# Layer 2's weight loads on GpSimd's queue, and two engines ordered by the scheduler, beside layer 1 of a three-stage kernel

## The chip, the cores and the metric

The kernel runs on one core of a Trainium2 chip. The core has five engines with an instruction stream of their own each: TensorE (PE in the rows: matmuls; PEld is its weight load), VectorE (DVE), ScalarE (ACT), GpSimd (POOL) and SyncE (SP). Each works through its stream in order. A DMA is put into a queue by an engine (here SyncE or GpSimd) and carried out beside them by the core's DMA engines. The metric is the device time of one execution in microseconds, as the median of three runs; a profile is one further execution.

## The reference

A retention (a linear attention with decay) feeds an expert layer with a gated activation, and that feeds a second expert layer with a rational activation. With the sizes: 4 batches, 8 heads, 768 positions, 64 per head, so 3072 tokens of 512; both layers go from 512 to 2048 and back.

```python
def _attn_ref(q, k, v):
    for t in range(S):
        state = gamma[None, :, None, None] * state + np.einsum('bhd,bhe->bhde', k[:, :, t], v[:, :, t])
        y[:, :, t] = scale * np.einsum('bhd,bhde->bhe', q[:, :, t], state)

def _moe_ref(x, w_in, w_out):            # layer 1
    h = x @ w_in
    g = h * (1.0 / (1.0 + np.exp(-1.702 * h)))
    return g @ w_out

def _moe2_ref(x, w_in, w_out, a, b):     # layer 2
    h = x @ w_in
    h2 = h * h
    P = a[0] + a[1] * h + a[2] * h2 + a[3] * h2 * h
    Q = 1.0 + np.abs(b[0]) * np.abs(h) + np.abs(b[1]) * h2
    return (P / (Q + 1e-06)) @ w_out
```

The inputs are 64-bit floats. The kernel makes a high and a low part of each matrix and adds three products (low times high, high times low, high times high) where the reference has one.

## The kernel before

Layer 1 goes over 6 blocks of 512 tokens, and in a block over 16 chunks f of 128 of the 2048 hidden columns: 96 steps. Step i, written in `step(i)`, does on TensorE first `g1(i+2)`, 12 matmuls into one of two banks hp (L1122), then `g2(i)`, 12 matmuls into four banks o that gather a whole block (L1143 to L1145). So g1 runs two steps ahead. Between them stand ScalarE's z=sigmoid(hp) (L1229), VectorE's z=hp*z (L1230), ScalarE's gh, the high part of z (L1238), and VectorE's gl, the low part (L1239). A bank hp is free again when VectorE's z has read it. After the 16th chunk, `evac` copies the four banks o into two pair tiles `os` (L1153, L1155) and SyncE stores them (L1156); layer 2 reads them back later.

Beside these steps runs other work, hung on the middle or the end of a step:

- Attention units for the chunks of 128 tokens that the later blocks read, 16 of them in steps 16 to 76. `att_unit` does the matmuls pY, pS and pK (L954), ScalarE and VectorE take pY out as xh and xl (L960, L962), VectorE makes the state st and the masked scores sm. What a unit needs is prepared before it: `load_raw` loads rawq, rawk and rawv (L735), `att_turn` scales and transposes q and k on VectorE (L816, L818) and writes them to DRAM as tq and tk (L823), `att_fetch` reads them back as qT and kT (L831). These DMAs, 4 or 2 for each of the seven tiles, are SyncE's. pY takes one of the two hp banks.
- The conversion of layer 2's weights: 32 units of 128 by 1024 words (512 KB), four for each of 8 groups g: u=4g and u+1 from w_in, u+2 and u+3 from w_out. `raw2(u)` loads the two 32-bit words of each number (L629, L631). `word2(u)` makes a 32-bit float of them: ScalarE u<-s (L561, in `w_first`), VectorE u<-u and s<-s (L567, L569), u<-u,s (L572) and u<-s,u (L583). For w_in four sums of quarter blocks follow on VectorE (L682). Each result is split by `split`: ScalarE takes the high part (L619), VectorE the low (L620), and `put` has GpSimd write both to DRAM, where layer 2 fetches them (L655 for w_in, L653 for w_out).

Which step a unit is converted in comes from `conv0`: group g begins at step 18 + 9g, less 0 to 4 for the last groups, and `conv2(g, x)` is called at the end of step i with x = i - conv0[g] from -1 to 9. It loads at x = -1, 0, 3 and 5, and the other pieces are spread over the ten steps.

Three pools set what may overlap. `ws` has 4 slots of 8 KB a partition, tag "s": a raw unit lies in one from its load to its put, the group's sums in one, one w_out result in one, and evac's two os pairs each in one. `ch` has 3, shared by z and the transposed q and k. The hp banks are 2.

The order on an engine is the program's where it is kept, and the scheduler's where not. In steps 14 to 77 TensorE, VectorE, ScalarE and SyncE keep the program's order:

```python
        with tc.manual_schedule(engines={E.PE, E.DVE, E.Activation, E.SP}):
            for i in range(FIRST_STEPS, XS0):   # 14 to 77
                step(i)
        for i in range(XS0, NS):                # 78 to 95
            step(i)
```

GpSimd, which only issues the puts there, is ordered by the scheduler. `behind(dma)` keeps one DMA in the program's order on its queue.

Of the kernel before, what the change touches and what calls it, by code (L numbers as in the profile page):

```python
# [18 lines left out]
P = 128  # L19
# [4 lines left out]
KD = DM // P  # L24
# [447 lines left out]
def tile_kernel(ctx: ExitStack, tc: tile.TileContext, q, k, v, w1i, w1o, w2i, w2o, pa, pb, cst, out):  # L472
    nc = tc.nc
# [47 lines left out]
    def unit(layer, u):  # L521
        return (ORD if layer == 1 else ORD2)[u]

    def stage_tag(u):

        if u < 16:
            at_slot = 31 - u
        elif u < 24:
            at_slot = 47 - u
        elif u < 28:  # L530
            at_slot = 55 - u
        elif u == 30:
            at_slot = 31
        else:
            return None
        return f"w{at_slot}"
# [49 lines left out]
    def w_high(layer, u, whole=True):  # L586
        nm, fc = unit(layer, u)
        if whole and layer == 1 and u in LATER:
            return
        m = STG[u]  # L590
        shape = [P, KD, P] if nm == "i" else [P, DM]
        if nm == "i":
            m = m.rearrange("p (c f) -> p c f", c=KD)
        pair = wp.tile([P, 2, *shape[1:]], F32R, tag=f"w{u}", name=f"w{nm}{layer}_{fc}")
        STG[u] = m
        W[layer, nm, fc] = (pair[:, 0], pair[:, 1])
        high = nc.scalar.copy(out=pair[:, 0], in_=m)
        if not whole:
            tc.keep_in_program_order(high)
# [9 lines left out]
    NG = KF // 2  # L609
# [3 lines left out]
    def behind(dma):  # L613

        tc.keep_in_program_order(dma)
# [6 lines left out]
    def raw2(u):  # L622

        nm, f = unit(2, u)
        src = {"i": w2i, "o": w2o}[nm].bitcast(I32)
        s = ws.tile([P, DM, 2], I32, tag="s", name=f"s2_{u}")
        if nm == "i":
            src = src[:, f * 2 * P : (f + 1) * 2 * P].rearrange("(c p) f -> p c f", p=P)
            behind(nc.sync.dma_start(out=s.rearrange("p (c f) t -> p c (f t)", c=KD), in_=src))  # L629
        else:  # L630
            behind(nc.sync.dma_start(out=s.rearrange("p f t -> p (f t)"), in_=src[f * P : (f + 1) * P, :]))  # L631
        STG[u] = RW[u] = s

    def word2(u):
        w_first(u)
        w_bits(u)
        w_sign(u, False)
# [4 lines left out]
    def parts(key, src, home):  # L642

        n = src.shape[1] // (2 * P)
        t = home.bitcast(F32R).rearrange("p a b -> p (a b)").rearrange("p (x h c) -> p x h c", x=n, h=2)
        split((t[:, :, 0], t[:, :, 1]), src.rearrange("p (x c) -> p x c", c=2 * P))
        OUT2[key] = t

    def put(key):
        t = OUT2.pop(key)  # L650
        g, x = key
        if x == "o":
            nc.gpsimd.dma_start(out=WO[g], in_=t.bitcast(F32))  # L653
        else:
            nc.gpsimd.dma_start(out=WC[g][x].rearrange("x p h k f -> p x (h k f)"), in_=t.rearrange("p x h c -> p x (h c)").bitcast(F32))  # L655

    def whole(f, src, home):
        t = home.bitcast(F32R).rearrange("p a b -> p (a b)").rearrange("p (h c) -> p h c", h=2)
        split((t[:, 0], t[:, 1]), src)
        OUT2[f, "o"] = t  # L660

    def conv2(g, x):

        u = 4 * g
        if x == -1:
            raw2(u)
        elif x == 0:
            raw2(u + 1)
            word2(u)
        elif x == 1:  # L670
            parts((g, 0), STG[u], RW.pop(u))
        elif x == 2:
            put((g, 0))
            word2(u + 1)
        elif x == 3:
            raw2(u + 2)
            a, b = STG.pop(u), STG.pop(u + 1)
            a11, a12, a21, a22 = a[:, : 2 * P], a[:, 2 * P :], b[:, : 2 * P], b[:, 2 * P :]
            t = SUM[g] = ws.tile([P, 4, 2 * P], F32, tag="s", name=f"sum{g}")
            A22S[g] = a22  # L680
            for y, p, q, op in ((0, a21, a22, ALU.add), (1, t[:, 0], a11, ALU.subtract), (2, a11, a21, ALU.subtract), (3, a12, t[:, 1], ALU.subtract)):
                nc.vector.tensor_tensor(out=t[:, y], in0=p, in1=q, op=op)  # L682
            parts((g, 1), t[:, 0:2].rearrange("p x c -> p (x c)"), RW.pop(u + 1))
        elif x == 4:
            put((g, 1))
        elif x == 5:
            raw2(u + 3)
            word2(u + 2)
            t = SUM.pop(g)
            parts((g, 2), t[:, 2:4].rearrange("p x c -> p (x c)"), RW.pop(u + 2))  # L690
            parts((g, 3), A22S.pop(g), t[:, 0:2])
        elif x == 6:
            put((g, 2))
            put((g, 3))
        elif x == 7:
            word2(u + 3)
            e = ws.tile([P, DM, 2], I32, tag="s", name=f"wo{2 * g}s")
            whole(2 * g, STG.pop(u + 2), e)
        elif x == 8:
            put((2 * g, "o"))  # L700
            whole(2 * g + 1, STG.pop(u + 3), RW.pop(u + 3))
        elif x == 9:
            put((2 * g + 1, "o"))
# [409 lines left out]
    def g1(j):  # L1113
        layer, bi, fc, t0, n = steps[j]
        hp = ps_h.tile([P, n], F32, tag="h", name=f"hp{j}")
        wh, wl = W[layer, "i", fc]
        xh, xl = X[layer, bi]
        terms = [(kk, w, x) for kk in range(KD) for w, x in ((wl, xh), (wh, xl), (wh, xh))]
        if j == 0:
            terms.sort(key=lambda t: ((t[2] is xl) + (t[1] is wl or t[2] is xl), t[0]))  # L1120
        for x, (kk, w, t) in enumerate(terms):
            nc.tensor.matmul(hp, w[:, kk, :], t[kk // 2][:, kk % 2, :], start=(x == 0), stop=(x == len(terms) - 1))  # L1122
        HP[j] = hp
# [90 lines left out]
    def load_wo(f):  # L1214
        t = WOT[f] = wp.tile([P, 2, DM], F32R, tag=f"w{14 + f}", name=f"wo{f}t")
        tc.keep_in_program_order(nc.sync.dma_start(out=t.bitcast(F32), in_=WO[f]))
# [7 lines left out]
    def act1_a(j):  # L1224
        n = steps[j][4]
        hp = HP.pop(j)
        z = ch.tile([P, n], F32, tag="z", name=f"z{j}")
        CH[j] = z
        nc.scalar.activation(out=z, in_=hp, func=ACTF.Sigmoid, scale=1.702)  # L1229
        nc.vector.tensor_tensor(out=z, in0=hp, in1=z, op=ALU.mult)  # L1230
# [54 lines left out]
    for u in range(NU):  # L1285
        t = stage_tag(u)
# [9 lines left out]
    E = mybir.EngineType  # L1296
    with tc.manual_schedule(engines={E.SP}):
# [207 lines left out]
        conv0 = [KF + 2 + 9 * g - (0, 0, 0, 0, 1, 2, 3, 4)[g] for g in range(NG)]  # L1505
# [13 lines left out]
        def x_piece(i):  # L1519
            left = 2  # L1520
            while xq and left and (xq[0][0] or i > XS0 + 8):
# [10 lines left out]
                else:  # L1532
                    left -= 1
                    for f in xr[s, kk][n]:
                        if f:
                            f()

        def step(i):
            nonlocal nxt, j
            while nxt < NS and nxt - lead[steps[nxt][0]] <= i:  # L1540
                j = nxt
                nxt += 1
                g1(j)
                act1_a(j)
            if 0 <= i - KF + 2 < WHOLE:
                w_high(1, LATER[i - KF + 2], False)
                w_low(1, LATER[i - KF + 2], False)
            if i == KF:
                tc.keep_in_program_order(nc.scalar.activation(out=ab[:, 6:7], in_=ab[:, 5:6], func=ACTF.Abs))
            late = [f() for f in todo[i][0]]  # L1550
            if j >= FIRST_STEPS + 2 and j in CH:
                act1_b(j)
            for f in late:
                if f:
                    f()
            g2(i)
            layer, bi, fc, t0, n = steps[i]
            if fc == KF - 1 and bi < 5:
                evac(bi)
            late = [f() for f in todo[i][1]]  # L1560

            if i >= XS0:
                x_piece(i)
            if i >= NS - 4:
                load_wo(2 * (i - NS + 4))
                load_wo(2 * (i - NS + 4) + 1)
            if i == XS0 + 4:
                for kk in range(2):
                    t = xp.tile([P, 2, 512], F32, tag=f"xh{kk}_0", name=f"xb{kk}")
                    XB.append(t)  # L1570
                    for c in range(2):
                        nc.sync.dma_start(out=t[:, c], in_=x2[4][2 * c + kk])
            for g in range(NG):
                x = i - conv0[g]
                if x == 9:
                    conv2(g, x)
            for g in range(NG):
                x = i - conv0[g]
                if -1 <= x < 9:
                    conv2(g, x)  # L1580
            for f in late:
                if f:
                    f()

        with tc.manual_schedule(engines={E.PE, E.DVE, E.Activation, E.SP}):
            for i in range(FIRST_STEPS, XS0):
                step(i)
        for i in range(XS0, NS):
            step(i)
# [32 lines left out]
```

## Time and profile before

| what | value |
|---|---|
| median of three runs | 1193.75 us (1192.49 to 1194.94) |
| the profiled execution | 1192.8 us, its span 1191.0 us, mean granted clock 0.971 |
| TensorE busy | 1119.5 us (94% of the span) |
| VectorE busy | 868.8 us (73%) |
| ScalarE busy | 655.2 us (55%) |
| GpSimd busy | 31.1 us (3%) |

The rows that matter stand in the section ahead of the prediction. A row of the stretches gives a window in microseconds from the span's start, its length, and what each engine was busy in it, then the granted TensorE clock as a share of full speed, the share of the DMA engines and GB/s. In the timeline, the figure in brackets is the time in which the engine was idle before the instruction, and what ended it. A wait lists who waited with which tile, for which engine's result or for which DMA, in total, how often, and the longest. Steps 16 to 77 of layer 1 lie between about 140 and 600 us; layer 2 begins past 680 us.

### The profile page before, as it was taken

The numbers are of one execution on the slowest core, as the hardware profiler recorded it, in microseconds if no ns is written. First come the engines' busy times: TensorE is split into PE (matmuls) and PEld (weight loads), VectorE is DVE, ScalarE is ACT, GpSimd is POOL, SyncE is SP. The second block draws the span as 40 slices with busy tenths as digits, with TensorE's granted clock in tenths as the row PEclk, the third lists the DMA queues.
The fourth block names the chain that finished last, engine by engine and source line by source line (L and its number), as shares of the span: only waits on it lengthen the run. The fifth ranks groups of instructions, "written<-read, shape, count | busy, mean of one in ns | idle before, by whom it ended". The sixth has DMA issues, their size and how long they took to land.

```text
span 1191.0 us, 18828 instructions
## 1 busy us (share of the span) xinstructions
PE 1119.5 (94%) x7217; PEld 911.8 (77%) x7217; DVE 868.8 (73%) x1192; ACT 655.2 (55%) x987; POOL 31.1 (3%) x52
## 2 busy tenths in 40 slices
PE   8999999698996879797999999999999999999998
PEld 6688878577775757586888888888888888888887
DVE  6999646375564445455577679999889899789895
ACT  5998322132232322222354569978778786787782
POOL 0000000000000000000000000000000000000000
PEclk9999999889998989899999999999999999999999
DMA  9944557565564554565278798583345561354100
GB/s 238 326 129 115 113 127 164 151 159 153 139 157 133 141 147 120 156 168 160 95 261 297 230 325 286 195 297 153 91 129 153 184 247 46 122 157 122 43 36 36
DMA packets 230394, 193.54 MB, mean 163 GB/s; under 512 B 153888, under 2 KB 178976, under 8 KB 230304
## 3 DMA queue, kind: packets, MB, share of 16 engines
q1 hardware_dynamic: 223904, 169.27, 49.4%
q0 software_dynamic: 6400, 23.07, 5.3%
q8 instruction: 57, 0.93, 0.3%
q14 instruction: 33, 0.27, 0.1%
HBM read 134.48 MB, written 57.67 MB: 161 GB/s over the span
## 4 chain that ended last, share of the span: by engine, by line
PE 66%; SPq 11%; DMA 9%; DVE 5%; issue 3%; ACT 2%; DVEq 0%; ACTq 0%
PE o L256 22%; PE hp L1122 13%; PE a L157 11%; SPq L735 7%; PE c L157 5%; DMA s<-in_moe_w_out_dram 4%; PE o L1143 3%; PE o L1144 3%; PE o L1145 3%; PE b L157 3%; DMA s<-in_moe_w_in_dram 2%; DMA xs<-x 2%; SPq L831 2%; SPq L823 1%; PE pY L954 1%
## 5 line engine op out<-in xcount | busy, mean ns | idle before, releaser
L1122 PE MATMUL hp<-xh,wi 128*128 128x512 f32 x768 | 266.7, 410 | 44.5 <-DVE z L1230 42.8
L1122 PEld LDWEIGHTS hp<-xh,wi 128*128 128x128 f32 x768 | 150.8, 196 | 81.8 <-DVE z L1230 45.9
L1122 PE MATMUL hp<-xl,wi 128*128 128x512 f32 x384 | 154.8, 404 | 0.0
L157 PE MATMUL a<-x,wi 128*128 128x512 f32 x576 | 145.3, 390 | 0.0
L1143 PE MATMUL o<-gh,wo 128*128 128x512 f32 x368 | 144.5, 393 | 0.0
L1144 PE MATMUL o<-gl,wo 128*128 128x512 f32 x368 | 143.6, 390 | 0.0
L1145 PE MATMUL o<-gh,wo 128*128 128x512 f32 x368 | 143.4, 390 | 0.0
L567 DVE TENSOR_SCALAR u<-u 128x512 f32<-128x512 f32 x64 | 27.0, 422 | 139.7 <-ACT u L561 139.7
L561 ACT ACTIVATE u<-s 128x512 f32<-128x512 f32 x64 | 43.1, 675 | 151.7 <-DMA s<-in_moe_w_in_dram 86.7
L157 PEld LDWEIGHTS a<-x,wi 128*128 128x128 f32 x576 | 108.0, 188 | 22.9 <-ACT b L180 0.4
L1238 ACT CAST gh<-z 128x512 fp32r<-128x512 f32 x80 | 49.6, 620 | 99.6 <-DVE z L1230 99.6
L1229 ACT ACTIVATE z<-hp 128x512 f32<-128x512 f32 x80 | 47.6, 595 | 86.3 <-PE hp L1122 80.1
L1230 DVE TENSOR_TENSOR z<-hp,z 128x512 f32<-128x512 f32 x80 | 54.9, 686 | 44.8 <-ACT z L1229 36.7
L1122 PEld LDWEIGHTS hp<-xl,wi 128*128 128x128 f32 x384 | 75.9, 198 | 15.2 <-issue 0.3
L320 DVE SCALAR_TENSOR_TENSOR z<-z,ab,w 128x1024 f32<-128x1024 f32 x48 | 61.6, 1283 | 28.4 <-ACT w L318 28.4
L1143 PEld LDWEIGHTS o<-gh,wo 128*128 128x128 f32 x368 | 69.7, 189 | 15.1 <-DVE wo L605 0.4
L1239 DVE TENSOR_TENSOR gl<-z,gh 128x512 fp32r<-128x512 f32 x80 | 54.7, 684 | 36.1 <-ACT gh L1238 35.0
L1144 PEld LDWEIGHTS o<-gl,wo 128*128 128x128 f32 x368 | 69.4, 189 | 14.6 <-DVE gl L1239 0.2
L1145 PEld LDWEIGHTS o<-gh,wo 128*128 128x128 f32 x368 | 69.2, 188 | 14.5
L157 PE MATMUL c<-x,wi 128*128 128x512 f32 x288 | 73.1, 389 | 0.0
L334 ACT ACTIVATE gh<-h 128x1024 fp32r<-128x1024 f32 x48 | 50.9, 1060 | 34.1 <-PE o L256 33.5
L338 DVE SCALAR_TENSOR_TENSOR gl<-h,gh 128x1024 fp32r<-128x1024 f32 x48 | 58.8, 1224 | 5.4 <-ACT gh L334 5.4
(246 smaller groups left out, 2203.5 us busy)
## 6 DMA issues: line engine op xcount, KB each, us to landing
wi<-wc SPq DMA_DIRECT2D x168, 256.0 KB, 2.9
s<-in_moe_w_in_dram SPq DMA_DIRECT2D x32, 512.0 KB, 5.6
s<-in_moe_w_out_dram SPq DMA_DIRECT2D x32, 512.0 KB, 5.2
x<-xc SPq DMA_DIRECT2D x28, 512.0 KB, 8.5
wc<-s POOLq DMA_DIRECT2D x24, 512.0 KB, 3.9
xc<-xo SPq DMA_DIRECT2D x36, 256.0 KB, 2.7
x<-os SPq DMA_DIRECT2D x20, 256.0 KB, 2.5
xs<-x SPq DMA_DIRECT2D x20, 256.0 KB, 4.3
```

The lines of the kernel that those rows point to most:

```text
L157: nc.tensor.matmul(bank, wt[:, a, k], XT[s, x, k][:, b], start=begin and y == 0, stop=y == 5, skip_group_check=True)
L256: nc.tensor.matmul(ACC[d], a[:, x, r], w[:, b], start=g == 0 and x == 0 and y == 0, stop=g == NG - 1 and x == 1 and y == 2)
L320: dve("q", [("ab", m)], lambda: stt(out=v["z"], in0=v["z"], scalar=ab[:, 6:7], in1=v["w"], op0=ALU.mult, op1=ALU.add))
L334: nc.scalar.activation(out=GT[m][0], in_=h, func=ACTF.Copy, scale=-1.0)
L338: nc.vector.scalar_tensor_tensor(out=gl, in0=h, scalar=-1.0, in1=gh.bitcast(F32), op0=ALU.mult, op1=ALU.subtract)
L735: nc.sync.dma_start(out=t[HALF[n], NP * x : NP * x + NP, :], in_=heads[x])
L1122: nc.tensor.matmul(hp, w[:, kk, :], t[kk // 2][:, kk % 2, :], start=(x == 0), stop=(x == len(terms) - 1))
L1143: nc.tensor.matmul(o, wl[:, r], gh, start=a, stop=False)
L1144: nc.tensor.matmul(o, wh[:, r], gl, start=False, stop=False)
L1145: nc.tensor.matmul(o, wh[:, r], gh, start=False, stop=z)
L1230: nc.vector.tensor_tensor(out=z, in0=hp, in1=z, op=ALU.mult)
L1239: nc.vector.tensor_tensor(out=gl, in0=z, in1=gh.bitcast(F32), op=ALU.subtract)
```

## The change

Three things change, all in steps 14 to 95 of layer 1.

1. `raw2` issues its DMA from GpSimd's queue, no longer from SyncE's. The load calls leave `conv2` and become `conv2_load(g, x)`, called where `conv2` was, at the end of a step.
2. The rest of `conv2` is called by `convert(i - 1)`, right after `g1` and `act1_a` of step i. What was written at the end of step i - 1 is so written early in step i.
3. VectorE and ScalarE leave the list of engines that keep the program's order in steps 14 to 77; the scheduler orders them there. TensorE and SyncE stay in the list.

```diff
@@ raw2
         if nm == "i":
-            behind(nc.sync.dma_start(out=s.rearrange("p (c f) t -> p c (f t)", c=KD), in_=src))
+            behind(nc.gpsimd.dma_start(out=s.rearrange("p (c f) t -> p c (f t)", c=KD), in_=src))
         else:
-            behind(nc.sync.dma_start(out=s.rearrange("p f t -> p (f t)"), in_=src[f * P : (f + 1) * P, :]))
+            behind(nc.gpsimd.dma_start(out=s.rearrange("p f t -> p (f t)"), in_=src[f * P : (f + 1) * P, :]))
@@
+    def conv2_load(g, x):
+        n = {-1: 0, 0: 1, 3: 2, 5: 3}.get(x)
+        if n is not None:
+            raw2(4 * g + n)
+
     def conv2(g, x):
         u = 4 * g
-        if x == -1:
-            raw2(u)
-        elif x == 0:
-            raw2(u + 1)
+        if x == 0:
             word2(u)
...
         elif x == 3:
-            raw2(u + 2)
...
         elif x == 5:
-            raw2(u + 3)
             word2(u + 2)
@@ enter
+        def convert(i):
+            for g in sorted(range(NG), key=lambda g: i - conv0[g] != 9):
+                if 0 <= i - conv0[g] <= 9:
+                    conv2(g, i - conv0[g])
+
         def step(i):
...
                 g1(j)
                 act1_a(j)
+            convert(i - 1)
...
             for g in range(NG):
-                x = i - conv0[g]
-                if x == 9:
-                    conv2(g, x)
-            for g in range(NG):
-                x = i - conv0[g]
-                if -1 <= x < 9:
-                    conv2(g, x)
+                conv2_load(g, i - conv0[g])
...
-        with tc.manual_schedule(engines={E.PE, E.DVE, E.Activation, E.SP}):
+        with tc.manual_schedule(engines={E.PE, E.SP}):
```

TensorE's order is the same in both kernels, and SyncE's is the same without the 32 loads. The number behind z, gh and hp is the step (z35 is that of step 35); u8 and s2_8 are unit 8 of the weights, wc2_0 and wo2 their places in DRAM, sum2 the sums of group 2.

GpSimd in the middle of group 2 (units 8 to 11), before: puts alone.

```order
L653 DMA wo2_137<-wo2s_3270 128x1024
L653 DMA wo3_138<-s2_7_3176 128x1024
L655 DMA wc2_0_111<-s2_8_3308 128x2x512
L655 DMA wc2_1_112<-s2_9_3447 128x2x512
L655 DMA wc2_2_113<-s2_10_3570 128x2x512
L655 DMA wc2_3_114<-sum2_3572 128x512
```

GpSimd at the same place, after:

```order
L653 DMA wo2_137<-wo2s_3286 128x1024
L629 DMA s2_8_3305<-in_moe2_w_in_dram 128x4x256
L629 DMA s2_9_3446<-in_moe2_w_in_dram 128x4x256
L653 DMA wo3_138<-s2_7_3176 128x1024
L655 DMA wc2_0_111<-s2_8_3305 128x2x512
L631 DMA s2_10_3570<-in_moe2_w_out_dram 128x1024
L655 DMA wc2_1_112<-s2_9_3446 128x2x512
L631 DMA s2_11_3758<-in_moe2_w_out_dram 128x1024
L655 DMA wc2_3_114<-sum2_3588 128x512
```

The loads of units 8 to 11 stand among the puts: that of unit 10 behind the put of unit 8, that of unit 11 behind the put of unit 9.

ScalarE from step 36 to 39, before: units 7 and 8 are begun two steps apart.

```order
L1238 CAST gh36_3248<-z36_3245 128x512
L561 ACTIVATE u7_3264<-s2_7_3176 128x512
L619 CAST wo2s_3270<-u6_3178 128x512
L1229 ACTIVATE z37_3286<-hp37_3273 128x512
L1238 CAST gh37_3289<-z37_3286 128x512
L619 CAST s2_7_3176<-u7_3264 128x512
L1229 ACTIVATE z38_3323<-hp38_3310 128x512
L1238 CAST gh38_3342<-z38_3323 128x512
L561 ACTIVATE u8_3449<-s2_8_3308 128x512
L960 CAST xh3_0_3092<-pY_13_3358 128x2x128
L960 CAST xh3_1_3093<-pY_13_3358 128x2x128
L1229 ACTIVATE z39_3478<-hp39_3465 128x512
```

ScalarE from step 34 to 35, after, where these units are now (a line of code has a number one higher from L1230 on in the changed file):

```order
L1230 ACTIVATE z34_3052<-hp34_3039 128x512
L561 ACTIVATE u7_3280<-s2_7_3176 128x512
L1239 CAST gh34_3072<-z34_3052 128x512
L561 ACTIVATE u8_3475<-s2_8_3305 128x512
L619 CAST s2_7_3176<-u7_3280 128x512
L961 CAST xh3_0_3092<-pY_12_3096 128x2x128
L961 CAST xh3_1_3093<-pY_12_3096 128x2x128
L561 ACTIVATE u9_3548<-s2_9_3446 128x512
L619 CAST s2_8_3305<-u8_3475 128x2x256
L1230 ACTIVATE z35_3201<-hp35_3188 128x512
L1239 CAST gh35_3214<-z35_3201 128x512
```

Units 7, 8 and 9 are begun within one step, and unit 9 ahead of z35. The same holds for VectorE, whose work on a unit follows ScalarE's: before, units are spread (u6 in step 34, u7 in 36, u8 in 38, u9 in 40); after, units 7 to 13 stand in steps 34 to 38, units 14 to 21 in 50 to 55, units 22 to 29 in 66 to 71 and units 0 to 6 in 18 to 24, and between these no unit stands.

## Rows read from the trace of the kernel before

**Rows 1.** Four stretches: engines' busy time, PEclk the granted clock, DMA share, GB/s.

```profile
160.00:600.00 440.00, 376.70 (x3294) 309.21 (x3293) 237.75 (x434) 118.30 (x223) 26.51 (x41) 0.92 0.56 147
600.00:690.00 90.00, 89.73 (x396) 73.89 (x395) 63.98 (x108) 44.16 (x76) 4.42 (x8) 1.00 0.77 268
235.00:241.00 6.00, 0.49 (x15) 0.30 (x7) 2.85 (x6) 1.21 (x3) 0.00 (x0) 0.50 0.43 147
241.00:244.00 3.00, 3.00 (x7) 2.42 (x8) 2.93 (x5) 1.62 (x4) 0.00 (x0) 0.50 0.19 44
```

**Rows 2.** Waits of the whole span: total us, times, longest us.

```profile
ACT u L561 <- DMA s<-in_moe_w_in_dram: 86.7, 7, 15.5
...
ACT u L561 <- DMA s<-in_moe_w_out_dram: 62.2, 11, 10.4
...
PE hp L1122 <- DVE z L1230: 42.8, 10, 9.6
...
PE pY L954 <- DVE z L1230: 17.2, 6, 4.1
...
PE pK L954 <- DMA rawv<-in_v_dram: 3.1, 1, 3.1
```

**Rows 3.** ScalarE's timeline: start us, duration us, operation, idle time before and its end.

```profile
237.39 0.66 ACT L561 ACTIVATE u<-s 128x512 f32<-128x512 f32 x1 [14.52 <-DMA s<-in_moe_w_in_dram]
237.95 0.58 ACT L1229 ACTIVATE z<-hp 128x512 f32<-128x512 f32 x1
```

**Rows 4.** SyncE's timeline: issue us, length us of the issues, tile and count.

```profile
216.71 1.78 SPq L823 DMA_DIRECT2D tq<-turnq  x4
...
232.64 1.09 SPq L629 DMA_DIRECT2D s<-in_moe_w_in_dram  x2
```

**Rows 5.** DMA issues of the page: count, KB each, median us to landing.

```profile
s<-in_moe_w_in_dram SPq DMA_DIRECT2D x32, 512.0 KB, 5.6
s<-in_moe_w_out_dram SPq DMA_DIRECT2D x32, 512.0 KB, 5.2
x<-xc SPq DMA_DIRECT2D x28, 512.0 KB, 8.5
wc<-s POOLq DMA_DIRECT2D x24, 512.0 KB, 3.9
```

**Rows 6.** TensorE's timeline: an attention unit, and a step without one.

```profile
596.24 1.15 PE L954 MATMUL pY<-qT,st 64*64 64x64 f32 x32
...
598.25 0.50 PE L1122 MATMUL hp<-xh,wi 128*128 128x512 f32 x1
...
603.83 0.39 PE L1122 MATMUL hp<-xh,wi 128*128 128x512 f32 x1
...
609.27 0.39 PE L1122 MATMUL hp<-xh,wi 128*128 128x512 f32 x1
```

**Rows 7.** The puts of L655 on GpSimd: duration ns min/median/max.

```profile
L655 POOL DMA_DIRECT2D wc<-s x24: 707/732/837, 173.1 to 632.3; - x24
```

**Rows 8.** Instructions by form, 150 to 620 us: count, busy us and mean ns, idle before.

```profile
L1230 DVE TENSOR_TENSOR z<-hp,z 128x512 f32<-128x512 f32 x64 | 43.9, 686 | 33.4 <-ACT z L1229 28.6 <-DMA kT<-tk 4.6
L1239 DVE TENSOR_TENSOR gl<-z,gh 128x512 fp32r<-128x512 f32 x64 | 43.7, 683 | 32.3 <-ACT gh L1238 31.6 <-PE o L1145 0.7
L572 DVE SCALAR_TENSOR_TENSOR u<-u,s 128x512 int32<-128x512 int32 x30 | 20.8, 692 | 1.0
...
L567 DVE TENSOR_SCALAR u<-u 128x512 f32<-128x512 f32 x30 | 12.7, 423 | 139.4 <-ACT u L561 139.4
L962 DVE TENSOR_TENSOR xl<-pY,xh 128x256 fp32r<-128x256 f32 x32 | 12.0, 417 | 0.0
...
L620 DVE TENSOR_TENSOR s<-u,s 128x512 fp32r<-128x512 f32 x15 | 10.3, 684 | 0.0
...
L818 DVE STREAM_TRANSPOSE turnk<-rawk 128x512 f32<-128x512 f32 x14 | 10.0, 711 | 0.5
...
L619 ACT CAST s<-u 128x512 fp32r<-128x512 f32 x15 | 9.2, 615 | 0.0
```

## The prediction, made before the changed kernel had run

> **What bounds the kernel now.** I read the stretches first. From 600 to 690 us TensorE is busy 89.73 of 90 us at a granted clock of 1.00; from 160 to 600 us, where layer 1 runs beside the attention units and the conversion of layer 2's weights, it is busy 376.70 of 440 us at 0.92 [rows 1]. So 63.3 us are lost there to idle time, and more to the clock. VectorE with 237.75 and ScalarE with 118.30 of these 440 us are far from full [rows 1]: the loss is one of order and of waiting. The waits say whose: TensorE waited 42.8 us with hp (L1122) and 17.2 us with pY for VectorE's z (L1230), and once 3.1 us for rawv; that is the 63 us. ScalarE waited 86.7 and 62.2 us at L561 for loads of layer 2's weights [rows 2]. The places join up on the timeline: at 237.39 ScalarE begins u<-s after 14.52 us idle behind the load, and z<-hp stands directly behind it in its in-order queue [rows 3]; around it, from 235 to 241 us, TensorE is busy 0.49 of 6 us [rows 1]. Why the load is late is in SyncE's queue: from 216.71 on it issues one attention unit's tq, tk, qT, kT, rawq, rawk and rawv, and the weight load comes last, at 232.64 [rows 4], 16 us later, though the load itself lands in 5.6 us and its w_out sister in 5.2 [rows 5]. The wait is the queue's, not the transfer's.
>
> The clock belongs to the same loss. From 235 to 241 us, when TensorE had next to nothing to do, the granted clock was 0.50 (1.2 of 2.4 GHz), and it stayed there from 241 to 244 us while TensorE was busy all the time [rows 1]. The mean of 0.92 from 160 to 600 us is about 70 us at half clock. In this long dip more than half of it fell on idle time; the shorter ones lie on busy work, and taking a third for all of them, some 47 us of busy time ran at half speed, which costs 24 us. Idle plus clock: 63 + 24 = **87 us** are there to be won, and each idle microsecond cost 0.38 more in clock. Steps without trouble show what is left: 5.44 us from one first matmul to the next (603.83, 609.27), and 2.0 us for an attention unit (596.24 to 598.25) [rows 6].
>
> **The change part by part.** The sum is made against the profiled run, 1192.8 us, of which 1191.0 are span; the median of the runs is 0.95 above it.
>
> (1) The 32 loads leave SyncE's queue, which has 32 entries fewer and is otherwise as before, and enter GpSimd's among its 48 puts. With it the 16 us row of attention DMAs no longer stands ahead of a load, and the 87 us lose their cause. What GpSimd needs to issue a load isn't shown; a put with the same bytes takes it 707 to 837 ns [rows 7], so 32 loads are some 25 us on an engine with 26.51 us of work in 440 [rows 1]: nothing. What a load takes to land from there isn't shown either. Bounds: a put from GpSimd of the same 512 KB, 3.9 us, and x<-xc, 512 KB in busier stretches of SyncE's queue, 8.5; I take 5.2, since the loads themselves took 5.2 to 5.6 in this traffic [rows 5]. The new risk is the order of that queue: a put waits for VectorE's low half, and the load behind it waits too (s2_10 stands behind the put of s2_8, s2_11 behind that of s2_9).
>
> The Trainium skill, page "SBUF — State Buffer", section "Who interferes with whom", speaks against this part: a DMA issued from GpSimd has descriptors that GpSimd writes through a port pair it shares with VectorE, a two-port VectorE operation locks it out, and the page advises to issue it from the queue of SP or ACT. Its warning gives about 620 ns alone and 3100 ns beside such an operation, which by an estimate from that page would be 2.5 us on each load and put. The trace shows no sign of it: 24 puts beside a busy VectorE spread over 0.13 us [rows 7], so the sum goes without it.
>
> (2) The conversion is called earlier in a step, with one step's delay; as SyncE's queue holds no load any more and the scheduler orders the two engines, this decides nothing by itself.
>
> (3) VectorE and ScalarE are ordered by the scheduler in steps 14 to 77. The instructions are the same, and TensorE's order is too. What moves is the place: before, a unit is converted every 2 to 3 steps from step 20 to 60 and on; after, seven or eight at a stretch, in steps 18 to 24, 34 to 38, 50 to 55 and 66 to 71, with none between. The ws slots make these bursts, since each evac takes two of the four. A step costs VectorE 0.69 us for z and 0.68 for gl; a group of four units four times (two TENSOR_SCALAR of 0.42, two SCALAR_TENSOR_TENSOR of 0.69), four half-width sums and a half-width split of 0.42 each, as xl is, and five splits of 0.69, 14.5 us or 3.6 a unit; an attention unit nine instructions from 0.42 (xl) to 0.71 (turn), 5.1 us by an estimate from these two ends [rows 8]. Counted along the new order, VectorE has 37 us of work in steps 34 to 38 and 49 us in 49 to 55 and 48 in 65 to 71, where TensorE has 5 x 5.44 + 2 x 2.0 = 31 us and 7 x 5.44 + 2 x 2.0 = 42 us [rows 6]: it falls 6 us behind in each, and 2 us in steps 18 to 25. About 5 us are forgiven, because g1 runs two steps ahead with two hp banks: ScalarE's 14.52 us [rows 3] cost TensorE 5.5 us from 235 to 241 [rows 1] and, as I read the gap just ahead of it, about 3 more. So VectorE alone would cost 1 to 2 us a burst.
>
> The slots come on top. A slot goes through load (5.2), conversion (about 4.2: 0.66 and 0.62 on ScalarE, 2.2 and 0.7 on VectorE [rows 3, 8]) and put (3.9); with the sum (about 9) and the wo pair (about 5) a group takes 67 us of slot time, 17 us on four slots, 4.2 us a unit, against 4.5 us (31/7) to 5.6 us of TensorE's time a unit. That leaves no room for the queueing of (1). ScalarE waits again at u<-s with xh and z behind it, now for a slot instead of SyncE. Walking each burst through the queues with these durations, I get TensorE idle 8.6 us in 49 to 55 and in 65 to 71, 7.6 in 33 to 38, 5 in 18 to 25, and 3.5 more there where attention units follow each other in under 16 us of SyncE's issuing; 33 in all, nothing after step 78. With the clock at 0.38: 33 x 1.38 = 46 us come back.
>
> Steps between the bursts have no conversion and should run like 603 us. All other stages are untouched.
>
> Sum: 1192.8 - 87 + 46 = 1151.8; against the median 1152.7, which I round to **1153 us**.
>
> **The rivals.**
>
> *Nearly all of the gain.* The slots keep pace, loads land like puts (3.9), and the 5 us of slack swallow VectorE's lag. Then idle time is 5 to 20 us, 7 to 28 with the clock: 1113 to 1134, say 1125. For it: 1.3 us less on each load is 1.3 us a group. Against: VectorE is over 100% occupied in three bursts.
>
> *The bursts eat it.* One us more on each load and each put is 2 us a unit, four units on four slots, 2 us a group; two groups a burst, four bursts: 16 us idle, 22 with the clock. At loads of 6.7 and puts of 5.4, 1.5 more each, that is 24 idle, 33 with the clock, 1186; at half of it 1169. For it: bursts move 1 MB (load and put) in less than 5 us, some 220 GB/s beside attention, where 268 GB/s was the busiest stretch shown [rows 1], and 8.5 us is seen for such transfers [rows 5].
>
> *Slower than before.* One mechanism: ScalarE's in-order wait for loads from GpSimd's queue, in the bursts, with z and xh behind it. It decides from the point where a slot's trip is 4 us longer (load plus put 13 instead of 9): 4 us a group, 32 idle more, 44 with the clock, 1197. At 5.5 us longer it is 1213. For: the put ahead of a load waits for VectorE, which is behind. Against: nothing in the trace over 8.5 for one such transfer. With the page's 2.5 us on load and on put alike, 5 us a trip, it would be 1208 by an estimate from it.
>
> *The queue was not it.* SyncE still issues 16 us for every unit, and TensorE might wait for rawv instead, as it did once for 3.1 us [rows 2]; if each of 14 units did, 43 us, 60 with the clock, 1213 with the rest as forecast. Against: once in 14 so far, and loads no longer take SyncE's turns.
>
> **How the numbers follow.** Forecast (1140 to 1170) 0.47; nearly all 0.20; eaten (1170 to 1191) 0.12, with another 0.05 that lands within 0.2% of 1193.75, which is about what a measurement of this kernel can tell from no change; slower by the slots 0.13; by SyncE 0.03. Faster 0.79, same 0.05, slower 0.16. The range leaves out 0.08 below and 0.11 above: 1125 to 1200.
>
> **What would show it.** Right: ScalarE's waits at L561 fall from 149 us to under 60; TensorE's waits for z from 60 to about 33, all of them in the four bursts; TensorE full and at clock 1.00 in steps 26 to 32, 40 to 48 and 57 to 64; VectorE full in the bursts; loads from GpSimd landing in about 5 us. Wrong: landings over 8 us, or issues on GpSimd over 2 us; waits for turn fetches or raw tiles on TensorE; gaps between the bursts; a granted clock that stays below 1.00 outside them.

## The result, and the profile after

The changed kernel takes 1156.57 us as the median of four runs (1153.43 to 1157.63), beside 1194.35 for the kernel before: a ratio of 0.968, with a 95% interval from 0.965 to 0.970. Forecast were 1153 us, in a range from 1125 to 1200. The profiled execution took 1157.04 us, of which 1155.3 are span: 35.7 less than before.

Eight stretches of the changed kernel, read as [rows 1]: the 440 us of that group, the whole piece from 130 us to the end of layer 1, two stretches between bursts of conversions, and the four bursts.

```profile
160.00:600.00 440.00, 407.45 (x3458) 333.70 (x3457) 262.15 (x479) 138.83 (x253) 49.51 (x76) 0.96 0.62 168
130.00:655.00 525.00, 490.94 (x3878) 401.98 (x3877) 316.57 (x566) 175.79 (x319) 52.48 (x80) 0.96 0.65 181
310.00:370.00 60.00, 60.00 (x505) 49.43 (x504) 27.50 (x46) 15.27 (x28) 0.00 (x0) 1.00 0.42 90
430.00:490.00 60.00, 60.00 (x604) 49.97 (x601) 31.63 (x58) 17.21 (x32) 3.32 (x5) 1.00 0.55 129
385.00:425.00 40.00, 32.56 (x244) 26.22 (x244) 29.14 (x56) 13.71 (x26) 8.30 (x14) 0.87 0.76 224
160.00:200.00 40.00, 33.04 (x314) 26.42 (x316) 29.08 (x57) 13.93 (x26) 7.87 (x12) 0.87 0.78 209
270.00:310.00 40.00, 32.12 (x244) 25.77 (x243) 28.73 (x54) 13.78 (x26) 7.91 (x12) 0.91 0.84 228
490.00:530.00 40.00, 34.31 (x256) 27.77 (x255) 29.97 (x58) 15.01 (x27) 9.10 (x14) 0.91 0.86 256
```

In both stretches between bursts TensorE is busy all the time at a granted clock of 1.00. Most of what is lost is lost in the four bursts: 7.4, 7.0, 7.9 and 5.7 us idle in the order of the rows, with a clock of 0.87 to 0.91. Some 3 us more are idle from 220 to 240 us, between the first two bursts, and 1.5 us at 627. From 130 to 655 us TensorE is idle 34.1 us; before, the same steps took from 130 to 690 us, with 63.6 us idle. Adding the stretches with a granted clock of 0.50, half of TensorE's busy time in each, gives 16.8 us after and 23.7 before. So the loss went from 87.3 to 50.9 us, 36.4 less, and the span got 35.7 shorter. I use this sum of idle time and clock for all runs below; it accounts for every span, against that of before, to about 2 us.

The waits after, from the whole span, read as [rows 2]: ScalarE's and VectorE's for the weight loads, and TensorE's for hp's two banks.

```profile
ACT u L561 <- DMA s<-in_moe_w_in_dram: 50.5, 15, 7.4
...
ACT u L561 <- DMA s<-in_moe_w_out_dram: 22.2, 10, 4.3
...
DVE s L569 <- DMA s<-in_moe_w_in_dram: 18.4, 7, 5.1
...
DVE s L569 <- DMA s<-in_moe_w_out_dram: 14.0, 7, 3.6
...
PE hp L1123 <- DVE z L1231: 15.6, 6, 4.7
...
PE hp L1123 <- DVE xl L963: 13.1, 5, 4.7
```

ScalarE's waits for loads are 72.7 us, where [rows 2] had 148.9. They are shorter and more: 25 for 18, the longest 7.4 for 15.5. And VectorE has waits of its own now, at L569, which had hardly any before.

How one such wait becomes idle time stands in the timeline of the burst at 397 us (GpSimd, then ScalarE, then TensorE). A put waited 6.17 us for VectorE's low half, the load behind it was issued at 397.38, ScalarE began that unit's u<-s at 405.33 after 4.27 us idle, xh<-pY came at 408.98, behind two splits and a second unit's u<-s (which had waited 1.25 us more for VectorE), and TensorE's next g1, which needs the bank that pY holds, came at 410.85 after 4.40 us idle.

```profile
396.69 0.71 POOL L655 DMA_DIRECT2D wc<-s  x1 [6.17 <-DVE s L620]
397.38 0.58 POOL L631 DMA_DIRECT2D s<-in_moe_w_out_dram  x1
```
```profile
405.33 0.67 ACT L561 ACTIVATE u<-s 128x512 f32<-128x512 f32 x1 [4.27 <-DMA s<-in_moe_w_out_dram]
...
408.98 0.64 ACT L961 CAST xh<-pY 128x256 fp32r<-128x256 f32 x2
```
```profile
410.85 0.77 PE L1123 MATMUL hp<-xh,wi 128*128 128x512 f32 x1 [4.40 <-DVE xl L963]
```

The loads and puts on GpSimd's queue, read as [rows 5], and the durations of the w_in loads' issues, read as [rows 7]:

```profile
wc<-s POOLq DMA_DIRECT2D x24, 512.0 KB, 4.1
...
s<-in_moe_w_in_dram POOLq DMA_DIRECT2D x16, 512.0 KB, 5.6
s<-in_moe_w_out_dram POOLq DMA_DIRECT2D x16, 512.0 KB, 6.1
```
```profile
L629 POOL DMA_DIRECT2D s<-in_moe_w_in_dram x16: 753/768/900, 139.0 to 517.8; - x16
```

### The profile page after: what moved, and what is told of

Read it like the earlier page. It is cut to its first block, busy times and chain, and to the rows that moved or that the text cites. A ratio compares the mean times of both kernels' runs of the same rounds, so it can differ in the third digit from the quotient of the medians.

```text
span 1155.3 us, 18810 instructions
## 1 busy us (share of the span) xinstructions
PE 1113.3 (96%) x7216; PEld 905.7 (78%) x7217; DVE 867.7 (75%) x1192; ACT 657.8 (57%) x987; POOL 52.7 (5%) x84
## 3 DMA queue, kind: packets, MB, share of 16 engines
q1 hardware_dynamic: 213152, 152.49, 46.5%
## 4 chain that ended last, share of the span: by engine, by line
PE 52%; issue 13%; DMA 6%; DVE 2%; POOL 1%; ACT 1%; SPq 0%; POOLq 0%; ACTq 0%; DVEq 0%
PE o L256 23%; PE a L157 11%; PE c L157 6%; PE hp L1123 4%; PE b L157 3%; DMA s<-in_moe_w_in_dram 2%; DMA s<-in_moe_w_out_dram 2%; PE o L1145 2%; PE o L1144 2%; PE o L1146 2%; DMA xs<-x 1%; DMA xc<-xo 1%; DMA wc<-sum 1%; POOL wc L655 0%; ACT u L561 0%
## 5 line engine op out<-in xcount | busy, mean ns | idle before, releaser
L1230 ACT ACTIVATE z<-hp 128x512 f32<-128x512 f32 x80 | 47.7, 596 | 118.5 <-PE hp L1123 101.2
L561 ACT ACTIVATE u<-s 128x512 f32<-128x512 f32 x64 | 43.4, 679 | 80.6 <-DMA s<-in_moe_w_in_dram 50.5
L1144 PEld LDWEIGHTS o<-gh,wo 128*128 128x128 f32 x368 | 69.8, 190 | 15.3 <-DVE wo L605 0.4
L334 ACT ACTIVATE gh<-h 128x1024 fp32r<-128x1024 f32 x48 | 50.9, 1060 | 34.1 <-PE o L256 33.3
L157 PEld LDWEIGHTS c<-x,wi 128*128 128x128 f32 x288 | 54.1, 188 | 11.2
```

The lines of the kernel that those rows point to most:

```text
L157: nc.tensor.matmul(bank, wt[:, a, k], XT[s, x, k][:, b], start=begin and y == 0, stop=y == 5, skip_group_check=True)
L334: nc.scalar.activation(out=GT[m][0], in_=h, func=ACTF.Copy, scale=-1.0)
L1144: nc.tensor.matmul(o, wl[:, r], gh, start=a, stop=False)
```

## The experiments

All ratios are to the kernel before, measured beside each run, with their 95% intervals. "Loss" is idle time plus clock from 130 us to the end of layer 1, as above.

| kernel | median us | ratio | loss us (idle + clock) |
|---|---|---|---|
| before | 1194.35 | 1 | 63.6 + 23.7 = 87.3 |
| changed | 1156.57 | 0.968 (0.965 to 0.970) | 34.1 + 16.8 = 50.9 |
| e1: loads on GpSimd alone | 1114.32 | 0.933 (0.931 to 0.936) | 5.3 + 3.1 = 8.4 |
| e4: scheduler alone | 1134.97 | 0.952 (0.948 to 0.956) | 22.4 + 4.6 = 27.0 |
| e2: changed, loads back on SyncE | 1136.72 | 0.952 (0.949 to 0.955) | 19.9 + 10.2 = 30.1 |
| e3: changed, program's order kept | 1119.00 | 0.937 (0.935 to 0.940) | 11.6 + 2.2 = 13.8 |
| e5: loads ahead of attention on SyncE | 1131.37 | 0.951 (0.948 to 0.953) | 18.2 + 7.8 = 26.0 |
| m_vector_kept | 1122.00 | 0.943 (0.940 to 0.946) | 12.4 + 2.9 = 15.3 |
| e8: VectorE without the low split | 1159.62 | 0.975 (0.972 to 0.978) | 39.0 + 13.3 = 52.3 |
| e9: half puts | 1150.95 | 0.968 (0.963 to 0.972) | 31.0 + 15.5 = 46.5 |
| p1: loads ahead of puts | 1156.55 | 0.970 (0.965 to 0.974) | 36.2 + 13.2 = 49.4 |
| t1: VectorE alone scheduled | 1186.81 | 0.994 (0.992 to 0.996) | 64.0 + 17.8 = 81.8 |
| t2: ScalarE alone scheduled | 1212.53 | 1.016 (1.011 to 1.021) | 81.9 + 26.2 = 108.1 |
| b2: e1 with rawv first | 1115.45 | 0.935 (0.932 to 0.937) | 7.6 + 1.5 = 9.1 |

### The change taken apart: e1, e2, e3, e4

The loads' queue alone (e1):

```diff
-            behind(nc.sync.dma_start(out=s.rearrange("p (c f) t -> p c (f t)", c=KD), in_=src))
+            behind(nc.gpsimd.dma_start(out=s.rearrange("p (c f) t -> p c (f t)", c=KD), in_=src))
...
-            behind(nc.sync.dma_start(out=s.rearrange("p f t -> p (f t)"), in_=src[f * P : (f + 1) * P, :]))
+            behind(nc.gpsimd.dma_start(out=s.rearrange("p f t -> p (f t)"), in_=src[f * P : (f + 1) * P, :]))
```

> The kernel before with the 32 weight loads on GpSimd's queue and nothing else: VectorE and ScalarE keep the program's order, so a unit is converted every 2 to 3 steps as before. If the place behind SyncE's 16 us of attention DMAs was the cause, the waits at L561 for loads fall from 149 us to under 60, no burst appears, and the time is 1115 to 1145, as good as the changed kernel or better. If the scheduler's order made the gain, this stays above 1180.

It is, with b2 below, the fastest kernel of the study: 1114.3 us, 42 below the changed kernel. The span is 1112.1 us, 78.9 less than before, of the 87 that could be won. Its waits for loads and its stretches:

```profile
PE pK L954 <- DMA rawv<-in_v_dram: 3.8, 2, 3.1
...
ACT u L561 <- DMA s<-in_moe_w_out_dram: 3.6, 3, 2.0
...
ACT u L561 <- DMA s<-in_moe_w_in_dram: 1.3, 2, 0.9
```
```profile
130.00:600.00 470.00, 464.98 (x3827) 383.12 (x3826) 309.46 (x551) 168.20 (x308) 52.00 (x80) 0.99 0.71 192
430.00:490.00 60.00, 59.94 (x500) 49.57 (x500) 40.01 (x72) 21.33 (x39) 7.76 (x12) 1.00 0.78 210
```

ScalarE waits 4.9 us for loads instead of 148.9, with the same conversions in the same places.

The other three parts: loads back on SyncE (e2), the program's order back (e3, the change of the `manual_schedule` line undone in the changed kernel), the scheduler alone (e4, that line alone changed in the kernel before).

> The changed kernel with the 32 loads back on SyncE's queue, where their place is kept; VectorE and ScalarE are still ordered by the scheduler, which then spreads the units (one every 2 to 3 steps, none of the bursts). If the loads' place was the cause, the loss stays: TensorE idle 50 us or more between 130 us and the end of layer 1, time 1175 to 1200. If the order of the two engines made the gain, it is 1150 to 1165.

> The changed kernel with VectorE and ScalarE back in the program's order: loads on GpSimd, conversion called one step later and early in the step. Differs from the loads-only kernel by that call alone. If the bursts are what is left of the loss (51 us of idle and clock in the changed kernel), this has a loss under 30 us and is at 1115 to 1140. If something else is left (SyncE's fetches, the slots), it is within 10 us of the changed kernel's 1157.

> The kernel before with VectorE and ScalarE ordered by the scheduler and nothing else; loads stay in SyncE's queue. If the loads' place is the cause, this brings little: 1180 to 1200, ScalarE or VectorE still waiting over 100 us for loads of s. If the scheduler's order makes the gain, 1150 to 1165.

e3 came out as the bursts' theory wanted, 1119 us; it is e1 with the conversion called one step later, and loses 5 us by that. e2 and e4 missed both of their ranges: I had expected the loads' place in SyncE's queue to keep the loss, and the scheduler alone brings 59 us with the loads left where they were. So each of the two parts alone gives more (79 and 59 us of span) than the whole change (36), which also has the later call. A kernel with the loads on GpSimd and the scheduler's order, but the conversion called where it was, was not run.

Where units are begun shows the bursts. These stretches, read as [rows 1], have ScalarE's u<-s (L561) alone, their number in brackets, in the third burst of the changed kernel, the gap behind it and the fourth burst:

```profile
370.00:422.00 52.00, 5.42 (x8) 0.90 0.84 238
422.00:478.00 56.00, 0.00 (x0) 1.00 0.46 109
478.00:528.00 50.00, 5.46 (x8) 0.93 0.89 251
```

in e3:

```profile
370.00:422.00 52.00, 2.65 (x4) 1.00 0.68 172
422.00:478.00 56.00, 3.29 (x5) 1.00 0.80 209
478.00:528.00 50.00, 2.64 (x4) 1.00 0.56 165
```

in e4:

```profile
370.00:422.00 52.00, 2.74 (x4) 1.00 0.64 169
422.00:478.00 56.00, 2.74 (x4) 1.00 0.70 183
478.00:528.00 50.00, 5.44 (x8) 0.97 0.72 218
```

Up to 478 us neither has a burst, nor have e1 and e2: with a kept queue or a kept engine the conversions are spread. The exception is the end: from 478 to 528 us e2 and e4 begin eight units, as densely as the changed kernel in its fourth burst, and e4 loses 6.2 of its 22.4 idle us there, from 505 to 520 us.

### One engine alone: t1, t2, m_vector_kept

In the kernel before, t1 (t2 has `{E.PE, E.DVE, E.SP}` there):

```diff
-        with tc.manual_schedule(engines={E.PE, E.DVE, E.Activation, E.SP}):
+        with tc.manual_schedule(engines={E.PE, E.Activation, E.SP}):
```

In the changed kernel, m_vector_kept:

```diff
-        with tc.manual_schedule(engines={E.PE, E.SP}):
+        with tc.manual_schedule(engines={E.PE, E.DVE, E.SP}):
```

> The kernel before with VectorE alone ordered by the scheduler; loads in SyncE's queue, ScalarE in the program's order. If the scheduler's gain with loads left on SyncE (1135) comes from ScalarE's u<-s standing later, behind z, this keeps the loss: 1175 to 1195. If it comes from VectorE's order, 1135 to 1150.

> The kernel before with ScalarE alone ordered by the scheduler; loads in SyncE's queue, VectorE in the program's order. ScalarE's u<-s stands up to 2 steps later for some units (u7 in step 37 for 36, u12 in 49 for 47). If that place is what the scheduler's gain comes from, 1130 to 1150; if VectorE's order is needed, above 1175.

> The changed kernel with VectorE back in the program's order and ScalarE alone ordered by the scheduler. Units are spread again (one in 1 to 3 steps, no burst). If the bursts are the loss, the time is 1115 to 1130, like the kernel with both engines kept (1119). If a scheduled ScalarE is at fault by itself, it stays above 1140.

With loads on SyncE, the scheduler's gain needs both engines: VectorE alone gives 0.6%, ScalarE alone makes it 1.6% slower, both give 4.8%. t1 kept the loss, as expected if ScalarE's order is needed, and t2 kept it, as expected if VectorE's is; that t2 would be slower than before was not expected. Who waits there shows why the loss was larger than one queue's issuing. These are SyncE's waits for the transpose, and VectorE's for ScalarE's u<-s, before:

```profile
SPq L823 <- DVE turnq L818: 131.2, 15, 15.4
```
```profile
DVE u L567 <- ACT u L561: 139.7, 15, 15.5
```

in t2, with ScalarE alone scheduled:

```profile
SPq L823 <- DVE turnq L818: 145.5, 15, 15.5
```
```profile
DVE u L567 <- ACT u L561: 110.2, 11, 16.7
```

in e4, with both scheduled:

```profile
SPq L823 <- DVE turnq L818: 56.3, 10, 9.5
```
```profile
DVE u L567 <- ACT u L561: 5.6, 11, 3.0
```

and in e1, with the loads on GpSimd:

```profile
SPq L823 <- DVE turnq L818: 61.2, 13, 8.1
```

The kernel before has a loop: a load behind SyncE's attention DMAs is late; ScalarE waits for it, VectorE waits for ScalarE; the transpose stands behind that conversion in VectorE's kept order; SyncE stands still for the transpose; and the next load stands behind it in SyncE's queue. The stretch ahead of [rows 4] is one turn of it (SyncE, then VectorE, before):

```profile
207.27 0.54 SPq L631 DMA_DIRECT2D s<-in_moe_w_out_dram  x1
216.71 1.29 SPq L823 DMA_DIRECT2D tq<-turnq  x3
```
```profile
211.92 0.43 DVE L567 TENSOR_SCALAR u<-u 128x512 f32<-128x512 f32 x1 [8.02 <-ACT u L561]
...
215.97 0.71 DVE L818 STREAM_TRANSPOSE turnq<-rawq 128x512 f32<-128x512 f32 x1
```

The load issued at 207.27 held VectorE until 211.92; the transpose behind it was done at 216.7; SyncE began its 16 us of attention DMAs then, and the next load came at 232.64. Either edit opens the loop: loads on GpSimd no longer stand behind SyncE's wait, and with both engines scheduled VectorE's wait for ScalarE's u<-s all but goes. With VectorE kept it goes on: in t2 VectorE waits 110.2 us for ScalarE. With ScalarE kept (t1) VectorE's wait goes as well, and yet SyncE waits 118.7 us for turnq, by another way round:

```profile
DVE u L567 <- ACT u L561: 4.4, 13, 1.4
...
DVE rawq L816 <- DMA rawq<-in_q_dram: 50.7, 11, 8.7
...
ACT s L619 <- DVE sum L682: 53.7, 6, 16.6
```

VectorE, in the scheduler's order, stands at the scaling of rawq until SyncE's load of rawq lands, and ScalarE, in the program's order, waits for the sums that VectorE has behind it, with xh and z behind those. At 384.51 SyncE issued rawq; VectorE had waited 8.71 us when it began at 389.61, and ScalarE 16.57 us at 394.38. In e4 the wait for rawq is 28.9 us. So a turn of the first loop and this second wait are seen in the traces; that they make all of the loss is argued from the sums of the waits.

m_vector_kept has loads on GpSimd and ScalarE scheduled; its units are spread, and it is at 1122 us. So a scheduled ScalarE is not at fault by itself, the bursts are. (VectorE alone scheduled, with loads on GpSimd, was not run.)

### Is it the place in SyncE's queue? e5

```diff
+            for g in range(NG):
+                conv2_load(g, i - conv0[g])
             late = [f() for f in todo[i][1]]
```

In the kernel before, with the loads taken out of `conv2` into `conv2_load` as in the change, but still on SyncE.

> The kernel before, loads still on SyncE's queue and all four engines in the program's order, but in each step the weight load is issued ahead of that step's attention DMAs. If the place in the queue was the cause, the time is 1115 to 1140 and GpSimd's queue isn't needed. If loads must leave SyncE's queue (it also stands still for VectorE's transposes), it stays above 1170; in between, both count.

1131.4 us: the place in the queue alone is worth 62 of the 79 us of span that GpSimd's queue brings. What is left has SyncE standing still with loads behind it, for the transpose and once for the put that frees a load's slot:

```profile
SPq L824 <- DVE turnq L819: 63.1, 12, 11.0
...
SPq L629 <- DMA wc<-sum: 14.8, 1, 14.8
```

with ScalarE waiting 53.7 us for loads (40.1 and 13.6), from 130 to 620 us. In e1 SyncE waits about as long for the transpose (61.2 us), but none of these loads stands behind it there.

### What makes the loss in the bursts: e8, e9, p1

The low split off VectorE (e8): ScalarE writes the high part into both halves, 1.05 us for 0.62, so the low parts are missing from the result.

```diff
-        split((t[:, :, 0], t[:, :, 1]), src.rearrange("p (x c) -> p x c", c=2 * P))
+        nc.scalar.copy(out=t, in_=src.rearrange("p (x c) -> p x c", c=2 * P).unsqueeze(2).to_broadcast([P, n, 2, 2 * P]))
...
-        split((t[:, 0], t[:, 1]), src)
+        nc.scalar.copy(out=t, in_=src.unsqueeze(1).to_broadcast([P, 2, DM]))
```

> The changed kernel without VectorE's low split of layer 2's weights: ScalarE writes the high part into both halves in one pass, so the low parts are missing from the result. The bursts stand as before. VectorE has 3.9 of 14.5 us less a group. If VectorE's occupancy makes the loss in the bursts, idle plus clock falls from 51 us to under 25 and the time to 1125 to 1133. If the slots' round trip of load, conversion and put makes it, only the shorter conversion shows: 40 to 48 us left, 1146 to 1154.

VectorE has 22 us less work from 130 us to the end of layer 1 (294.1 for 316.6), and the loss is 52.3 us, for 50.9. The same burst as above, in e8 and then in e1:

```profile
385.00:425.00 40.00, 32.87 (x248) 26.27 (x248) 26.35 (x49) 16.71 (x26) 7.90 (x12) 0.91 0.77 231
```
```profile
385.00:425.00 40.00, 40.00 (x398) 33.18 (x397) 26.95 (x50) 12.79 (x24) 5.69 (x9) 1.00 0.66 165
```

With 26.35 us of VectorE's work in 40 TensorE loses 7 us in one, and with 26.95 us nothing in the other. So VectorE's occupancy alone isn't the cause. The edit isn't clean, though, and the time lies above both of the ranges expected: ScalarE has 18.7 us more (194.5 for 175.8), 3 of them in this stretch, and TensorE's waits for xl, which follows ScalarE's xh, rose from 13.1 to 24.6 us. What VectorE's lighter work gave back may have been lost there.

Half puts (e9): the high halves alone are written, and layer 2 reads them twice, so the low parts are missing.

```diff
-            nc.gpsimd.dma_start(out=WO[g], in_=t.bitcast(F32))
+            nc.gpsimd.dma_start(out=WO[g][:, 0], in_=t[:, 0].bitcast(F32))
...
-            nc.sync.dma_start(out=t.bitcast(F32), in_=WC[g][w // 2][w % 2])
+            nc.sync.dma_start(out=t.bitcast(F32), in_=WC[g][w // 2][w % 2][:, 0].unsqueeze(1).to_broadcast([P, 2, 2, P]))
```

> The changed kernel with puts of the high halves alone (256 KB for 512), which layer 2 then reads twice, so the low parts are missing. VectorE's work and the bursts stand as before. If the slots' round trip makes the loss, a put that lands 1.5 to 2 us earlier gives 12 to 16 us of idle time, 17 to 22 with the clock: 1135 to 1140. If VectorE's occupancy makes it, the time stays within 4 us of 1157.

The ratio is that of the changed kernel, and the loss 46.5 us for 50.9. Inconclusive: the puts landed only little earlier,

```profile
wc<-s POOLq DMA_DIRECT2D x24, 256.0 KB, 3.5
```

3.5 us for 4.1, not 1.5 to 2 us as I had assumed. The loads landed earlier too, in 5.1 and 5.2 us for 5.6 and 6.1. At 1.1 to 1.5 us a trip and 8 groups the round trip, counted as in the prediction, would give some 9 to 12 us of idle time; 3.1 were seen, in the slower of two executions that lie 5.9 us apart. That speaks for neither reading.

Loads ahead of puts (p1): GpSimd's queue in the program's order, the loads called before `convert(i - 1)`.

```diff
-        with tc.manual_schedule(engines={E.PE, E.SP}):
+        with tc.manual_schedule(engines={E.PE, E.SP, E.Pool}):
...
+            for g in range(NG):
+                conv2_load(g, i - conv0[g])
             convert(i - 1)
```

> The changed kernel with GpSimd's queue kept in the program's order and each load written ahead of the conversions of its step, so that a load stands right behind the put that frees its slot and no longer behind puts that wait for VectorE's low half (s2_10 ahead of the put of s2_8). The bursts stand as before. If the loads' place behind waiting puts makes the loss in the bursts, idle plus clock falls from 51 us to 20 to 30 and the time to 1125 to 1137. If the slots' round trip itself makes it, 45 us or more are left: 1150 to 1160.

No gain: 1156.6 us, loss 49.4. A load now stands right behind the put that frees its slot, and waits for that put to land:

```profile
POOL s L629 <- DMA wc<-s: 40.9, 8, 6.5
...
POOL s L631 <- DMA wc<-s: 36.4, 7, 6.4
```

Where the changed kernel had 14.3 and 9.8 us of these, p1 has 77.3 together, and ScalarE and VectorE wait as long for loads as before or longer (48.9, 27.0, 25.7 and 15.2 us from 130 to 655 us). So taking loads from behind a put that waits for VectorE, as in the timeline at 397 us, doesn't win the time back; without that wait the load waits for the slot. But the puts landed later here, in 6.0 us for 4.1, which may have eaten a part of what the order gave. The result fits the round trip of the slots as the limit of a burst. It isn't isolated: no run changes the number of slots.

### The rest of e1: b2

```diff
+            if FLAT < c and c + 2 <= LASTC:
+                load_raw(c + 2, "v")
             if c + 2 <= LASTC:
                 att_fetch(c + 2)
             if c + 3 <= LASTC:
                 load_raw(c + 3, "q")
                 load_raw(c + 3, "k")
-            if FLAT < c and c + 2 <= LASTC:
-                load_raw(c + 2, "v")
```

> The loads-only kernel (1114) with rawv's DMAs issued ahead of the turn fetches and of rawq and rawk in SyncE's queue. What the loads-only kernel still lost was 5.3 us idle and 3.1 us of clock after 206 us, of which 3.8 us was TensorE waiting for rawv. If that goes, 1106 to 1111; if the later qT and kT take its place as the wait, no better than 1114.

1115.5 us, loss 9.1 for 8.4: another fetch takes rawv's place (TensorE waits 4.6 us once for kT), and nothing is won; by their intervals the two kernels can't be told apart.

## Why the prediction was right, and where it wasn't

The direction, the size (1153 forecast, 1156.6 measured) and the range were right. By its steps:

- **87 us to be won.** Right: the loss before was 87.3 us by this sum, and e1 wins 78.9 of them with the loads' queue alone.
- **The cause of the late load.** Right as far as it went: e5, which changes that place alone, wins 62 us. SyncE's 16 us of issuing is one half; the other is that SyncE stands still for the transpose, which stands behind the conversion that waits for the load. The prediction saw one turn's issuing and not the loop, and so couldn't see that the scheduler alone would also open it.
- **33 us of idle time come back.** 34.1 measured. By place: 8.1 and 2.7 in the first burst and behind it (5 and 3.5 forecast; the 2.7 are waits for rawv at 234 us, where attention units follow each other), 7.9 in the second (7.6), 7.4 in the third (8.6), 5.7 in the fourth (8.6), 1.5 at 627 us (0). That the total is so near is partly luck: 3 us too little in the first burst and 4 too much in the last two cancel, and the walk that gave them counted with a full VectorE, which it wasn't.
- **0.38 us of clock for each us idle.** Too small: 16.8/34.1 = 0.49. This term, 4.3 us, is most of the 5 us by which the sum, 46 against 50.9, was short. It isn't a constant of this kernel: it was 0.21 in e4 (4.6/22.4) and 0.59 in e1 (3.1/5.3).
- **VectorE falls behind in the bursts.** Wrong as a reason. The count was 49 us of work against 42 of TensorE; in the bursts it was busy 28.7 to 30.0 us in 40, waiting for loads itself, and e8 took work off it without a gain (though with more for ScalarE). Work counted by instructions put between two z's of the new order isn't work in that time, since the steps stretch.
- **The slots make the bursts.** Half right. The same pools with VectorE or both engines kept (m_vector_kept, e3) have none, and with the loads in SyncE's kept queue (e2) there is one, from 478 to 528 us. In these runs it takes both freedoms; the slots' own part was not varied.
- **Loads land in 5.2, puts in 3.9.** Nearly: 5.6 and 6.1, and 4.1. The 5.2 to 5.6 of [rows 5] was a misreading, since half of each of those groups of 32 are layer 1's own weights; read by line, layer 2's loads had landed in 4.9 (w_in) and 4.7 us (w_out). GpSimd's issuing cost nothing, as forecast: 753 to 900 ns for a w_in load, 554 to 591 for a w_out load.
- **The rule on GpSimd's DMAs beside VectorE.** The Trainium skill, page "SBUF — State Buffer", section "Who interferes with whom", has a DMA from GpSimd held up by VectorE's two-port operations; by an estimate from the 620 and 3100 ns of its section "A bandwidth-pool intuition that's wrong (but worth ruling out)" that is 2.5 us each. The runs show less. With spread conversions, loads from GpSimd landed in 5.7 and 5.8 us (e1), and those from SyncE in medians of 4.9 and 4.7 (before) or 4.3 (e5): 0.8 to 1.5 us apart, and no issue in e1 took over 0.9 us. Whether that difference is the rule's or the traffic's is not shown.
- **ScalarE's waits under 60 us.** 72.7, and 32.4 more on VectorE, where the prediction looked for none. TensorE's waits, forecast as 33 us for z, were 16.2 for z and 13.1 for xl.
- **The rivals.** None took over, but the bursts' price was real: 38 us against e3, which differs by the kept order alone, and 42 against e1. The prediction's own sum had it: without the 46 us the bursts bring, the loads alone would have been at 1107. It named that price and didn't ask what the kernel would be without the third part.

What stays open is how the loss in the bursts divides between the slots' round trip and the order in which ScalarE and VectorE wait for loads ahead of xh and z. VectorE's work alone isn't it (e8 beside e1), and the loads' place behind waiting puts doesn't decide it (p1), but each of these two edits lengthened another piece of the trip.

## What to carry to other kernels

Two edits that each free a kernel from the same loop needn't add up: here 79 and 59 us alone were 36 in the kernel with both and the later call, where the scheduler packed the conversions into bursts. Where a queue stands still, follow the wait once around, from the late DMA to the engine that waits, to what stands behind it there, and back to the queue; it could be cut at several places here (79, 62 and 59 us), but freeing one of two coupled engines did not cut it. Count how densely a new order packs the side work before taking its engine for free, and run the parts apart.

## What the runs showed of the hardware

Loads of the same 512 KB landed in medians of 4.9 to 6.3 us from GpSimd's queue (changed kernel, e1, e3, m_vector_kept) and of 4.3 to 5.7 from SyncE's (before, e2, e4, e5). In e1 a w_in load took 753 to 900 ns to issue on GpSimd and a w_out load 574 to 588; on SyncE, before, 378 to 603 and 347 to 580. Neither kept e1 from being the fastest. The puts of 256 KB in e9 landed in 3.5 us, those of 512 KB in the changed kernel in 4.1.
